# First pair reordered, third pair's words on ScalarE's queue, w_out's low bits through PSUM

## The chip, the cores and the metric

The kernel runs on one core of one Trainium2 chip. The metric is device time in microseconds of one execution; for the kernel before it is 912.71 us, the median of three runs (912.54 to 913.43). The engines are TensorE (PE, with its weight loads as PEld), VectorE (DVE), ScalarE (ACT), GpSimd (POOL) and SyncE (SP). SP and ACT also issue DMAs, each through a queue of its own.

## The reference, cut to what matters

Routed attention over 4 batches, 8 heads, 768 positions and 64 dimensions: each query and key is assigned to the nearest of 16 centroids of its head, and a query sees the keys of its own centroid only. Its output is the input of a two-layer block with a squared ReLU.

```python
q_assign = np.argmax(np.einsum('bhsd,hcd->bhsc', q_n, c_n), axis=-1)
k_assign = np.argmax(np.einsum('bhsd,hcd->bhsc', k_n, c_n), axis=-1)
mask = q_assign[:, :, :, None] == k_assign[:, :, None, :]
scores = np.where(mask, scale * np.matmul(q, k.transpose(0, 1, 3, 2)), -1e9)
x = attn @ v                       # bridge: (B,H,S,D) -> (3072, 512)
h = x @ w_in                       # 512 x 2048
out = np.square(np.maximum(h, 0)) @ w_out   # 2048 x 512
```

## The kernel before, in words

**Order.** Until the end of the first output tile the program is under a manual schedule: every engine works in the order in which the code is written, so the place of a call is its place in the engine's queue. A DMA issue stands in the queue of the engine that issues it, and waits there for what it needs.

**Attention.** Two heads make a pair, and 16 pairs (NG) are worked one after the other in the loop over `p`. For a pair, q and k are turned so that the head dimension lies on partitions (`qkT`), logits against the centroids give a number for each position, and these become rows (`ohT`) that a matmul turns into the mask. A pair has nine tiles: `mask` (L435) and `score` (L426) accumulate in one PSUM tile, `exponential` (L442) reads it on ScalarE, VectorE adds the tiles into `total` (L445), and `times_v` (L459) multiplies by v into the banks V and M (`av_a`, `av_b`). `add_up` (L478) sums `total` for the normalization. PSUM holds three `sc` tiles of two banks each, plus V and M.

How q and k are turned differs. Pairs 0 and 1 are turned on TensorE (L265 in `turn_first`, L282 in `turn`, with ScalarE and VectorE copying out of PSUM). From pair 2 on, `split_words` (L302) copies q and k on ScalarE into `flat`, a DMA (L303) writes them to DRAM as words, and a transposing DMA (L314, `turn_words`) brings them back. Pair 0 also has its one-hot rows turned on TensorE (L386 in `turn_onehot`), copied by ScalarE (L394) and VectorE (L396); later pairs send their numbers through DRAM (L370, L373) into `rows`, two buffers that are filled with zeros at the start (L218).

**Head.** Loads are issued first: pair 0's q on SP and its k on ACT behind the centroids, then pairs 1 and 2 and v on SP. GpSimd makes an identity, TensorE runs eight warm-up matmuls on it (L171), VectorE makes small constants and fills, `centroids_norm` (L226 to L245) prepares the centroids, pair 0 is turned, `centroids_turned` (L251, L254) turns the centroids, and the logits follow (L322).

**The two products.** The batches are worked in the order 1, 2, 3, 0. `up` multiplies by w_in: eight tiles of rows of the hidden layer, each with seven products (L742, four records each) by a Strassen-like scheme. `combine` runs them in the order 1, 6, 2, 7, 5, 4, 3, each into a PSUM bank: the first is copied out by ScalarE (L705), the others are added by VectorE (L699) or subtracted (L522). The sums of w_in that the scheme needs, `w_s`, are made by GpSimd (L542, L522) two tiles ahead. `down` multiplies by w_out in the same manner (L794), three tiles of columns per batch.

**Rounding.** Each weight block of 128 x 512 is loaded as 64-bit words and rounded in three steps. `round_1` on ScalarE makes the absolute value (L130) and the low bits (L131), which it writes over the low half of the loaded words. `round_2` on VectorE joins sign and low bits (L137), limits the value (L140) and shifts (L144). `round_3` on GpSimd adds both (L152). Blocks 0 to 14 (w_in) are done in the attention loop, block 15 and the 16 blocks of w_out inside the first `up`, three per tile: `Rounding.prepare` issues `round_1` for the next tile's blocks behind the copy of a tile's first product, and `Rounding.between` issues `round_2` and `round_3` behind the additions of products 6, 7 and 3. `up` and `down` share eight PSUM banks (`banks`).

Of the kernel before, what the change touches and what calls it, by code (L numbers as in the profile page):

```python
# [25 lines left out]
def kernel(  # L26
# [101 lines left out]
    def round_1(i):  # L128
        dst, lo, hi = of_block(i)
        nc.scalar.activation(out=dst.bitcast(F32), in_=hi.bitcast(F32), func=ACT.Abs)  # L130
        nc.scalar.activation(  # L131
            out=lo.bitcast(F32), in_=lo, func=ACT.Copy, bias=2.0, scale=2.0 ** -51
        )

    def round_2(i):
        dst, lo, hi = of_block(i)
        nc.vector.scalar_tensor_tensor(  # L137
            out=lo, in0=hi, scalar=0x80000000, in1=lo, op0=ALU.bitwise_and, op1=ALU.bitwise_or
        )
        nc.vector.tensor_scalar(  # L140
            out=hi.bitcast(F32), in0=dst.bitcast(F32), scalar1=2.0 ** -15, scalar2=HIGHEST,
            op0=ALU.max, op1=ALU.min,
        )
        nc.vector.tensor_scalar(  # L144
            out=dst, in0=hi, scalar1=3, scalar2=None, op0=ALU.logical_shift_left
        )
# [9 lines left out]
    load_qk(0, (nc.sync, nc.scalar))  # L156
    for pair in range(1, BY_PE + 1):
        load_qk(pair)
# [7 lines left out]

    ident = const.tile([P, P], F32, name="ident")
    make_identity(nc, ident)
    warm_up = ps_sc.tile([P, 2, 512], F32, name="sc")
    for _ in range(8):  # L170
        nc.tensor.matmul(warm_up[:, 0, 0:P], lhsT=ident, rhs=ident, start=True, stop=True)  # L171
# [45 lines left out]
    for t in rows_of:  # L217
        nc.vector.memset(t, 0.0)  # L218
# [31 lines left out]
    def centroids_turned():  # L250
        nc.tensor.transpose(  # L251
            out=M[:, 0:P], in_=cn.rearrange("p e d -> p (e d)"), identity=ident
        )
        nc.vector.tensor_copy(out=cnT, in_=M[:, 0:P])  # L254
# [4 lines left out]
    def turn_first(which):  # L259
        if which == 0:  # L260
            qkT[0] = qktp.tile([P, 2 * NCH, P], F32, name="qkT")
        pt = ps_sc.tile([P, 2, 512], F32, name="sc")
        for c in range(NCH):
            for e in range(2):
                nc.tensor.matmul(  # L265
                    pt[D * e : D * (e + 1), c // NB, (c % NB) * P : (c % NB + 1) * P],
                    lhsT=raw[0][which][:, e, c], rhs=ident, start=True, stop=True,
                )
        for i in range(2):
            copy = nc.vector.tensor_copy if which and i else nc.scalar.copy  # L270
            c = NCH * which + NB * i
            copy(out=qkT[0][:, c : c + NB].rearrange("p c n -> p (c n)"), in_=pt[:, i, 0:TB])
        if which == 1:
            raw.pop(0)
# [19 lines left out]
    def split_words(pair, which):  # L294
        if pair >= NG:
            return
        if which == 0:
            words[pair] = dram.tile([2 * NCH, P, 2, 2 * D], U16, name="words")
        flat = loads.tile([P, NCH, 2, 2 * D], U16, name="flat", tag="qk")
        src = raw[pair][which].bitcast(U16).rearrange("p h c (d two) -> p h c two d", two=2)  # L300
        for e in range(2):
            nc.scalar.copy(out=flat[:, :, :, D * e : D * (e + 1)], in_=src[:, e])  # L302
        nc.sync.dma_start(  # L303
            words[pair][NCH * which : NCH * (which + 1)].rearrange("c p two d -> p c two d"),
            flat,
        )
        if which == 1:
            raw.pop(pair)
# [69 lines left out]
    def turn_onehot():  # L378
# [4 lines left out]
        po = sc.pop("oh").rearrange("p a n -> p (a n)").bitcast(BF16)[:, 0 : NBL * P]  # L383
        po = po.rearrange("p (b g i) -> p b g i", b=NBL, g=4)
        for b in range(NBL):
            nc.tensor.transpose(  # L386
                out=po[:, b].rearrange("p g i -> p (g i)"),
                in_=oh[:, b].rearrange("p e c -> p (e c)"), identity=ident_b,
            )
        for which in range(2):  # L390
            dst = ohT[0][:, which].rearrange("p (g b i) -> p b g i", g=2, b=NBL)
            src = po[:, :, 2 * which : 2 * which + 2]
            if which == 0:
                nc.scalar.copy(out=dst, in_=src)  # L394
            else:
                nc.vector.tensor_scalar(  # L396
                    out=dst, in0=src, scalar1=BIG, scalar2=-BIG, op0=ALU.mult, op1=ALU.add
                )

# [164 lines left out]
    turn_first(0)  # L564
    turn_first(1)
    centroids_turned()
    logits(0, begin("ls"))
# [7 lines left out]
    for p in range(NG):  # L575
# [17 lines left out]
        if p == 0:  # L593
# [3 lines left out]
            split_words(2, 0)  # L597
            turn_onehot()
            turn(1, 2, V)
# [20 lines left out]
        if p == 0:  # L620
            split_words(2, 1)
            turn_words(2)
        split_words(p + 3, 0)
# [8 lines left out]
        if p:  # L632
            finish(p - 1)
            round_2(p - 1)
            round_3(p - 1)
        split_words(p + 3, 1)
# [30 lines left out]
    banks = fast.enter_context(tc.tile_pool(name="banks", bufs=8, space=PSUM, reuse_waits="tile"))  # L667
# [161 lines left out]
    class Rounding:  # L829
# [5 lines left out]
        def prepare(self, i):  # L835
            for n in self.of(i) + self.of(1) if i == 0 else self.of(i + 1):
                if n >= N_IN:
                    round_1(n)

        def between(self, i, j):  # L840
            n = dict(zip((6, 7, 3), self.of(i))).get(j)
            if n is not None:
                round_2(n)
                round_3(n)
                load_ahead(n + 1)
            elif (i, j) in SUMS:
# [221 lines left out]
```

## Time and profile before

| | |
|---|---|
| median of three runs | 912.71 us (912.54 to 913.43) |
| profiled execution: its own time, its span | 913.43 us, 911.6 us |
| PE busy | 899.4 us of the span |
| DVE, ACT, POOL busy | 581.7, 316.2, 150.1 us |
| logits of pair 0 (L322) | start at 10.09 us |
| first mask (L435) | starts at 17.49 us |
| first up (L742) | 321.44 to 398.83 us |
| a later up | 471.66 to 543.90 us |

Times of events count from the start of the span, which is that of one profiled execution; the span leaves out what lies around the first and the last instruction. A row of the timeline gives the start and the duration in us, the engine, the line, what is written from what, and in brackets how long the engine had been idle before and what ended it. Granted TensorE clock is 1.000 in the records of the whole span; the spacing of matmuls shows speed directly.

### The profile page before, as it was taken

The numbers are of one execution on the slowest core, as the hardware profiler recorded it, in microseconds if no ns is written. First come the engines' busy times: TensorE is split into PE (matmuls) and PEld (weight loads), VectorE is DVE, ScalarE is ACT, GpSimd is POOL, SyncE is SP. The second block draws the span as 40 slices with busy tenths as digits, with TensorE's granted clock in tenths as the row PEclk, the third lists the DMA queues.
The fourth block names the chain that finished last, engine by engine and source line by source line (L and its number), as shares of the span: only waits on it lengthen the run. The fifth ranks groups of instructions, "written<-read, shape, count | busy, mean of one in ns | idle before, by whom it ended". The sixth has DMA issues, their size and how long they took to land.

```text
span 911.6 us, 11728 instructions
## 1 busy us (share of the span) xinstructions
PE 899.4 (99%) x4543; PEld 578.8 (63%) x4543; DVE 581.7 (64%) x930; ACT 316.2 (35%) x457; POOL 150.1 (16%) x168
## 2 busy tenths in 40 slices
PE   8999999999999999899999999999999999999997
PEld 5444444444444455478875568886558887557886
DVE  5798888888888999994326565225655333656321
ACT  5876677776776567530001110001110000111000
POOL 0000100001000267710023310023220003240000
PEclk9999999999999999999999999999999999999999
DMA  7677778777673154110000000000000000000000
GB/s 261 154 191 220 218 214 208 179 210 213 172 177 86 61 184 139 41 70 24 24 24 0 1 0 19 18 19 16 1 1 0 24 24 24 0 1 0 24 24 27
DMA packets 98482, 75.03 MB, mean 82 GB/s; under 512 B 54666, under 2 KB 89074, under 8 KB 98162
## 3 DMA queue, kind: packets, MB, share of 16 engines
q1 hardware_dynamic: 91474, 64.33, 24.9%
q10 hardware_dynamic: 6944, 9.86, 3.4%
q8 instruction: 38, 0.62, 0.3%
q14 instruction: 26, 0.21, 0.1%
HBM read 43.83 MB, written 19.34 MB: 69 GB/s over the span
## 4 chain that ended last, share of the span: by engine, by line
PE 92%; DVE 5%; issue 1%; ACT 1%; POOL 0%; DVEq 0%; POOLq 0%
PE bank L794 32%; PE bank L742 28%; PE sc L426 12%; PE av_a L459 9%; PE av_b L459 4%; PE sc L435 3%; PE sc L322 1%; DVE w_raw L137 1%; PE sc L478 1%; DVE g L699 1%; DVE w_raw L140 1%; DVE total L445 1%; DVE xT L510 0%; PE sc L171 0%; PE sc L265 0%
## 5 line engine op out<-in xcount | busy, mean ns | idle before, releaser
L699 DVE TENSOR_TENSOR g<-bank,g 128x384 f32<-128x384 f32 x192 | 102.9, 553 | 90.8 <-PE bank L742 88.6
L442 ACT ACTIVATE ex<-sc 128x1024 f32<-128x1024 f32 x144 | 144.2, 1025 | 39.0 <-PE sc L426 34.1
L426 PE MATMUL sc<-qkT 64*128 64x512 f32 (+1 forms) x768 | 150.6, 484 | 0.0
L794 PE MATMUL bank<-w_out,g 128*128 128x256 f32 x576 | 127.2, 379 | 0.0
L794 PEld LDWEIGHTS bank<-w_out,g 128*128 128x128 f32 x576 | 109.4, 190 | 15.7
L699 DVE TENSOR_TENSOR osb<-bank,osb 128x256 f32<-128x256 f32 x72 | 29.3, 422 | 136.5 <-PE bank L794 125.9
L742 PE MATMUL bank<-x_t,w_s 128*128 128x384 f32 x256 | 93.3, 487 | 3.1 <-POOL w_s L522 3.1
L742 PE MATMUL bank<-xT,w_in 128*128 128x384 f32 x256 | 93.2, 487 | 0.0
L742 PE MATMUL bank<-xT,w_s 128*128 128x384 f32 x256 | 93.0, 486 | 0.0
L426 PEld LDWEIGHTS sc<-qkT 64*128 64x128 f32 x768 | 65.9, 188 | 41.9 <-issue 30.1
L794 PE MATMUL bank<-w_t,g_s 128*128 128x256 f32 x384 | 86.8, 379 | 0.0
L794 PE MATMUL bank<-w_t,g 128*128 128x256 f32 x384 | 86.8, 379 | 0.0
L459 PE MATMUL av_a<-ex,v_raw 128*64 128x512 f32 x384 | 85.9, 596 | 0.0
L542 POOL TENSOR_TENSOR w_s<-w_in 128x256 f32<-128x256 f32 x32 | 26.7, 835 | 351.3 <-PE bank L794 235.4
L445 DVE TENSOR_TENSOR total<-total,ex 128x1024 f32<-128x1024 f32 x64 | 78.7, 1229 | 6.5
L705 ACT COPY osb<-bank 128x256 f32<-128x256 f32 x12 | 4.5, 372 | 216.1 <-PE bank L794 216.1
L794 PEld LDWEIGHTS bank<-w_t,g_s 128*128 128x128 f32 x384 | 73.0, 190 | 9.9
L794 PEld LDWEIGHTS bank<-w_t,g 128*128 128x128 f32 x384 | 73.0, 190 | 9.9
L705 ACT COPY g<-bank 128x384 f32<-128x384 f32 x32 | 15.3, 477 | 173.9 <-PE bank L742 173.9
L742 PEld LDWEIGHTS bank<-x_t,w_s 128*128 128x128 f32 x256 | 48.4, 190 | 37.9 <-POOL w_s L522 4.8
L152 POOL TENSOR_TENSOR w_in<-w_in,w_raw 128x512 int32<-128x512 int32 x16 | 22.1, 1378 | 296.4 <-DVE w_in L144 296.4
L742 PEld LDWEIGHTS bank<-xT,w_s 128*128 128x128 f32 x256 | 48.6, 190 | 33.9
(128 smaller groups left out, 1021.5 us busy)
## 6 DMA issues: line engine op xcount, KB each, us to landing
words<-flat SPq DMA_DIRECT2D x28, 384.0 KB
w_raw<-in_moe_w_in_dram SPq DMA_DIRECT2D x16, 512.0 KB
w_raw<-in_moe_w_out_dram SPq DMA_DIRECT2D x16, 512.0 KB
v_raw<-in_v_dram SPq DMA_DIRECT2D x16, 384.0 KB
rb<-far_r SPq DMA_DIRECT2D x32, 192.0 KB
out_dram<-osb SPq DMA_DIRECT2D x23, 256.0 KB
k_raw<-in_k_dram ACTq DMA_DIRECT2D x13, 384.0 KB
q_raw<-in_q_dram ACTq DMA_DIRECT2D x12, 384.0 KB
```

Source lines behind the costliest of these rows:

```text
L137: nc.vector.scalar_tensor_tensor(out=lo, in0=hi, scalar=0x80000000, in1=lo, op0=ALU.bitwise_and, op1=ALU.bitwise_or)
L152: nc.gpsimd.tensor_tensor(out=dst, in0=dst, in1=lo, op=ALU.add)
L426: nc.tensor.matmul(sc[i][:, e, cols], lhsT=qkT[pair][rows, NCH + c], rhs=qkT[pair][rows, n.start // P : n.stop // P], start=first, stop=no ...
L435: nc.tensor.matmul(sc[i][:, e, cols], lhsT=ohT[pair][rows, 1, c * P : (c + 1) * P], rhs=ohT[pair][rows, 0, columns(i)], start=first, stop= ...
L442: nc.scalar.activation(out=ex[i], in_=sc.pop(i), func=ACT.Exp, scale=SCALE)
L445: eng.tensor_tensor(out=out, in0=a, in1=b, op=ALU.add)
L459: nc.tensor.matmul(bank[D * e : D * (e + 1), 0 : n.stop - n.start], lhsT=raw_v[pair][:, e, c], rhs=ex[i][:, e, cols], start=c == 0, stop=c ...
L542: nc.gpsimd.tensor_tensor(out=s1, in0=a[1][0], in1=a[1][1], op=ALU.add)
L699: nc.vector.tensor_tensor(out=out, in0=bank, in1=to, op=ALU.add)
L705: nc.scalar.copy(out=c11, in_=bank)
L742: nc.tensor.matmul(bank, lhsT=operands[j][0][:, kk], rhs=operands[j][1][:, kk], start=(kk == 0), stop=(kk == H2 - 1),)
L794: nc.tensor.matmul(bank, lhsT=left[:, f], rhs=right[:, f], start=(f == 0), stop=(f == F2 - 1))
```

## The change

- Loads: pair 0's k is issued on SP behind its q; ACT issues only the centroids there.
- Warm-up: six matmuls on a tile of zeros that VectorE fills, before the identity is made.
- Turning of pair 0: in four halves with a bank for each (V, M, and one of each of two `sc` tiles), the centroids' turning between the two halves of k.
- Fills of `rows`: moved behind `turn_onehot` on VectorE.
- One-hot rows: two halves in two banks, the first copied out by ScalarE for both q and k, the second by VectorE.
- Pair 2's words: both copies behind the first six exponentials, their DMAs issued by ACT; pair 3's first half moves behind the last three exponentials of pair 0.
- w_out's low bits: written by ScalarE into a tile of a pool of two PSUM banks (`lows`), read there by `round_2`; the bits of block n + 2 are issued behind `round_3` of block n. Six banks are left in `banks`.

```diff
--- before.py
+++ after.py
@@ -125,17 +125,26 @@
         dst = weights[i][0] if i < N_IN else w_out[:, i - N_IN]
         return dst.bitcast(U32), raw_w[i][:, :, 0], raw_w[i][:, :, 1]
 
-    def round_1(i):
+
+    low = {}
+
+    def round_1(i, bits=True):
         dst, lo, hi = of_block(i)
         nc.scalar.activation(out=dst.bitcast(F32), in_=hi.bitcast(F32), func=ACT.Abs)
+        if bits:
+            round_bits(i, lo.bitcast(F32))
+
+    def round_bits(i, out):
+        low[i] = out
         nc.scalar.activation(
-            out=lo.bitcast(F32), in_=lo, func=ACT.Copy, bias=2.0, scale=2.0 ** -51
+            out=out, in_=of_block(i)[1], func=ACT.Copy, bias=2.0, scale=2.0 ** -51
         )
 
     def round_2(i):
         dst, lo, hi = of_block(i)
         nc.vector.scalar_tensor_tensor(
-            out=lo, in0=hi, scalar=0x80000000, in1=lo, op0=ALU.bitwise_and, op1=ALU.bitwise_or
+            out=lo, in0=hi, scalar=0x80000000, in1=low.pop(i).bitcast(U32),
+            op0=ALU.bitwise_and, op1=ALU.bitwise_or,
         )
         nc.vector.tensor_scalar(
             out=hi.bitcast(F32), in0=dst.bitcast(F32), scalar1=2.0 ** -15, scalar2=HIGHEST,
@@ -153,8 +162,7 @@
 
     cen = once.tile([P, D], F32, name="cen")
     nc.scalar.dma_start(cen, centroids.rearrange("h c d -> (h c) d"))
-    load_qk(0, (nc.sync, nc.scalar))
-    for pair in range(1, BY_PE + 1):
+    for pair in range(BY_PE + 1):
         load_qk(pair)
     load_v(0)
 
@@ -164,11 +172,13 @@
         tc.manual_schedule(engines={E.PE, E.DVE, E.Activation, E.Pool, E.SP})
     )
 
+    zeros = once.tile([P, P], F32, name="zeros")
+    nc.vector.memset(zeros, 0.0)
+    warm_up = ps_sc.tile([P, 2, 512], F32, name="sc")
+    for _ in range(6):
+        nc.tensor.matmul(warm_up[:, 0, 0:P], lhsT=zeros, rhs=zeros, start=True, stop=True)
     ident = const.tile([P, P], F32, name="ident")
     make_identity(nc, ident)
-    warm_up = ps_sc.tile([P, 2, 512], F32, name="sc")
-    for _ in range(8):
-        nc.tensor.matmul(warm_up[:, 0, 0:P], lhsT=ident, rhs=ident, start=True, stop=True)
     ident_b = const.tile([P, P], BF16, name="ident_b")
     nc.vector.tensor_copy(out=ident_b, in_=ident)
     ups = const.tile([P, D], F32, name="ups")
@@ -214,8 +224,6 @@
     marks = once.tile([P, 3, 32], BF16, name="marks")
     nc.vector.memset(marks, 0.0)
     rows_of = [once.tile([P, 2, S], BF16, name=f"rows_{i}") for i in range(2)]
-    for t in rows_of:
-        nc.vector.memset(t, 0.0)
 
     cnT = const.tile([P, H * C], F32, name="cnT")
     cn = const.tile([P, 2, D], F32, name="cen_n")
@@ -248,29 +256,28 @@
             )
 
     def centroids_turned():
+        turned = warm_up[:, 1, 0:P]
         nc.tensor.transpose(
-            out=M[:, 0:P], in_=cn.rearrange("p e d -> p (e d)"), identity=ident
-        )
-        nc.vector.tensor_copy(out=cnT, in_=M[:, 0:P])
+            out=turned, in_=cn.rearrange("p e d -> p (e d)"), identity=ident
+        )
+        nc.vector.tensor_copy(out=cnT, in_=turned)
 
     qkT = {}
     ohT = {}
 
-    def turn_first(which):
-        if which == 0:
+
+    def turn_first(which, i, bank, copy):
+        if which == 0 and i == 0:
             qkT[0] = qktp.tile([P, 2 * NCH, P], F32, name="qkT")
-        pt = ps_sc.tile([P, 2, 512], F32, name="sc")
-        for c in range(NCH):
+        for c in range(NB):
             for e in range(2):
                 nc.tensor.matmul(
-                    pt[D * e : D * (e + 1), c // NB, (c % NB) * P : (c % NB + 1) * P],
-                    lhsT=raw[0][which][:, e, c], rhs=ident, start=True, stop=True,
+                    bank[D * e : D * (e + 1), c * P : (c + 1) * P],
+                    lhsT=raw[0][which][:, e, NB * i + c], rhs=ident, start=True, stop=True,
                 )
-        for i in range(2):
-            copy = nc.vector.tensor_copy if which and i else nc.scalar.copy
-            c = NCH * which + NB * i
-            copy(out=qkT[0][:, c : c + NB].rearrange("p c n -> p (c n)"), in_=pt[:, i, 0:TB])
-        if which == 1:
+        c = NCH * which + NB * i
+        copy(out=qkT[0][:, c : c + NB].rearrange("p c n -> p (c n)"), in_=bank[:, 0:TB])
+        if which == 1 and i == 1:
             raw.pop(0)
 
     def turn(pair, part, bank):
@@ -291,7 +298,7 @@
 
     words = {}
 
-    def split_words(pair, which):
+    def split_words(pair, which, queue=nc.sync):
         if pair >= NG:
             return
         if which == 0:
@@ -300,7 +307,7 @@
         src = raw[pair][which].bitcast(U16).rearrange("p h c (d two) -> p h c two d", two=2)
         for e in range(2):
             nc.scalar.copy(out=flat[:, :, :, D * e : D * (e + 1)], in_=src[:, e])
-        nc.sync.dma_start(
+        queue.dma_start(
             words[pair][NCH * which : NCH * (which + 1)].rearrange("c p two d -> p c two d"),
             flat,
         )
@@ -380,22 +387,30 @@
         ohT[0] = spare.rearrange("p a n -> p (a n)")[:, 0 : 2 * S].rearrange(
             "p (a n) -> p a n", a=2
         )
-        po = sc.pop("oh").rearrange("p a n -> p (a n)").bitcast(BF16)[:, 0 : NBL * P]
-        po = po.rearrange("p (b g i) -> p b g i", b=NBL, g=4)
-        for b in range(NBL):
-            nc.tensor.transpose(
-                out=po[:, b].rearrange("p g i -> p (g i)"),
-                in_=oh[:, b].rearrange("p e c -> p (e c)"), identity=ident_b,
-            )
-        for which in range(2):
-            dst = ohT[0][:, which].rearrange("p (g b i) -> p b g i", g=2, b=NBL)
-            src = po[:, :, 2 * which : 2 * which + 2]
-            if which == 0:
-                nc.scalar.copy(out=dst, in_=src)
-            else:
-                nc.vector.tensor_scalar(
-                    out=dst, in0=src, scalar1=BIG, scalar2=-BIG, op0=ALU.mult, op1=ALU.add
+
+        for half, bank in enumerate((sc.pop("oh")[:, 0], M)):
+            n = NBL // 2
+            blocks = slice(n * half, n * (half + 1))
+            po = bank.bitcast(BF16)[:, 0 : n * P].rearrange("p (b g i) -> p b g i", b=n, g=4)
+            for b in range(n):
+                nc.tensor.transpose(
+                    out=po[:, b].rearrange("p g i -> p (g i)"),
+                    in_=oh[:, n * half + b].rearrange("p e c -> p (e c)"), identity=ident_b,
                 )
+            for which in range(2):
+                dst = ohT[0][:, which].rearrange("p (g b i) -> p b g i", g=2, b=NBL)[:, blocks]
+                src = po[:, :, 2 * which : 2 * which + 2]
+                if half == 0:
+                    nc.scalar.activation(
+                        out=dst, in_=src, func=ACT.Copy,
+                        **({"scale": BIG, "bias": -BIG} if which else {}),
+                    )
+                elif which:
+                    nc.vector.tensor_scalar(
+                        out=dst, in0=src, scalar1=BIG, scalar2=-BIG, op0=ALU.mult, op1=ALU.add
+                    )
+                else:
+                    nc.vector.tensor_copy(out=dst, in_=src)
 
 
 
@@ -561,9 +576,12 @@
             loaded += 1
 
     centroids_norm()
-    turn_first(0)
-    turn_first(1)
+    turn_first(0, 0, V, nc.scalar.copy)
+    turn_first(0, 1, M, nc.scalar.copy)
+    halves = [ps_sc.tile([P, 2, 512], F32, name="sc")[:, 0] for _ in range(2)]
+    turn_first(1, 0, halves[0], nc.scalar.copy)
     centroids_turned()
+    turn_first(1, 1, halves[1], nc.vector.tensor_copy)
     logits(0, begin("ls"))
     for i in ("oh", 0, 1):
         begin(i)
@@ -594,8 +612,9 @@
             for i in range(2):
                 turn(1, i, (V, M)[i])
                 score(p, i, 0, True)
-            split_words(2, 0)
             turn_onehot()
+            for t in rows_of:
+                nc.vector.memset(t, 0.0)
             turn(1, 2, V)
             for i in range(NB):
                 if i == 2:
@@ -618,9 +637,11 @@
             tile_of(p, i)
             add(nc.vector, first, first, ex[i])
         if p == 0:
-            split_words(2, 1)
+            for i in range(2):
+                split_words(2, i, nc.scalar)
             turn_words(2)
-        split_words(p + 3, 0)
+        else:
+            split_words(p + 3, 0)
 
 
         for i in range(NCH, NCH + NB):
@@ -633,6 +654,8 @@
             finish(p - 1)
             round_2(p - 1)
             round_3(p - 1)
+        if p == 0:
+            split_words(3, 0)
         split_words(p + 3, 1)
         load_qk(p + 4, (nc.scalar, nc.scalar))
         round_1(p)
@@ -664,7 +687,8 @@
 
     w_out = w_out_pool.tile([P, FT, DM], F32, name="w_out")
     fast = ExitStack()
-    banks = fast.enter_context(tc.tile_pool(name="banks", bufs=8, space=PSUM, reuse_waits="tile"))
+    banks = fast.enter_context(tc.tile_pool(name="banks", bufs=6, space=PSUM, reuse_waits="tile"))
+    lows = fast.enter_context(tc.tile_pool(name="lows", bufs=2, space=PSUM, reuse_waits="tile"))
     outp = fast.enter_context(tc.tile_pool(name="outp", bufs=2, reuse_waits="tile"))
     gp = fast.enter_context(tc.tile_pool(name="gp", bufs=1, reuse_waits="tile"))
 
@@ -835,7 +859,13 @@
         def prepare(self, i):
             for n in self.of(i) + self.of(1) if i == 0 else self.of(i + 1):
                 if n >= N_IN:
-                    round_1(n)
+                    round_1(n, False)
+                    if n < N_IN + 2:
+                        self.bits(n)
+
+        def bits(self, n):
+            if n < N_IN + FT:
+                round_bits(n, lows.tile([P, NW], F32, name="low"))
 
         def between(self, i, j):
             n = dict(zip((6, 7, 3), self.of(i))).get(j)
@@ -843,6 +873,8 @@
                 round_2(n)
                 round_3(n)
                 load_ahead(n + 1)
+                if n >= N_IN:
+                    self.bits(n + 2)
             elif (i, j) in SUMS:
                 w_out_sum(SUMS[i, j])
 
```

## The prediction

> **What bounds the kernel now.** I read the page first, then the chain of waits, then the timeline of the two stretches that the diff touches.
>
> ```profile
> PE 899.4 (99%) x4543; PEld 578.8 (63%) x4543; DVE 581.7 (64%) x930; ACT 316.2 (35%) x457; POOL 150.1 (16%) x168
> ...
> PE 92%; DVE 5%; issue 1%; ACT 1%; POOL 0%; DVEq 0%; POOLq 0%
> ```
>
> TensorE is busy for 899.4 of 911.6 us, so an edit elsewhere pays only where TensorE stands still, or runs slowly. The chain of waits shows the first such stretch, the head:
>
> ```profile
> 1.36 3.78 PE sc L171 x16
> 5.14 3.51 PE sc L265 x48
> 8.68 0.49 ACT qkT L272
> 9.19 0.56 DVE qkT L272
> 9.74 0.21 DVE cnT L254
> ...
> 10.09 0.85 PE sc L322 x8
> ...
> 14.58 1.57 ACT flat L302 x2
> 16.14 0.71 ACT ex L394
> 16.88 0.57 DVE ex L396
> 17.49 0.61 PE sc L435 x4
> ```
>
> Warm-up, turning of the first pair, copies and logits (L322) follow one another; then ScalarE's two copies of L302 stand ahead of the one-hot copy that the first mask (L435) waits for. From 17.49 on, the chain stays on TensorE with only short issue gaps.
>
> The second stretch is the first w_in product (up), from 321.44 to 398.83 us. The chain gives a later one as its measure:
>
> ```profile
> 471.66 72.24 PE bank L742 x224
> ```
>
> The first takes 398.83 - 321.44 = 77.39 us, 0.78 of it L478, so it loses 77.39 - 0.78 - 72.24 = 4.4 us. The timeline shows how:
>
> ```profile
> 378.46 1.28 POOL L152 TENSOR_TENSOR w_out<-w_out,w_raw 128x512 int32<-128x512 int32 x1 [2.09 <-DVE w_out L144]
> 378.76 1.53 DVE L137 SCALAR_TENSOR_TENSOR w_raw<-w_raw 128x512 uint32<-128x512 uint32 x1
> 378.89 1.45 PE L742 MATMUL bank<-xT,w_in 128*128 128x384 f32 x4
> 379.70 1.17 POOL L542 TENSOR_TENSOR w_s<-w_in 128x256 f32<-128x256 f32 x1
> 380.33 0.83 DVE L140 TENSOR_SCALAR w_raw<-w_out 128x512 f32<-128x512 f32 x1
> ...
> 381.79 1.56 PE L742 MATMUL bank<-x_t,w_s 128*128 128x384 f32 x4 [1.45 <-POOL w_s L522]
> ```
>
> L137 takes 0.68 us where GpSimd is idle, and 1.53 here beside L152; L140 takes 0.43 alone and 0.83 here. VectorE and GpSimd hold each other up, w_s comes late, and TensorE waits (two waits, 3.1 us in all).
>
> **The change, part by part: warm-up and first turning.** TensorE now multiplies zeros that VectorE fills, not the identity that GpSimd makes (wait until 1.36). The other engines' first work begins at 0.74; a fill like L175 takes 0.11 us, so TensorE can start near 0.95. The 16 passes of L171 took 3.78 us, 0.236 each; six matmuls are 12 passes, 2.83 us, and end at 3.8. By slices of 0.1 us, the queue of the first q load carries its last packet between 3.7 and 3.8. So the old warm-up kept TensorE away from data that was there for 1.3 us, and the new one ends as it arrives. I let the turning start at 3.9.
>
> Clock: L265's passes come 0.105 us apart until about 6.3 (five us after TensorE began) and the 24 of k 0.062 apart. With the switch left at 6.3, q's 24 passes end at 6.4. The k half is 12 x 0.062 = 0.74, to 7.14; the centroids' transpose to about 7.4; the other half to 8.14. **A rule speaks against this:** the Trainium skill (TensorE: Matmul & The Clock Gate, Part 1) says that full clock needs about 3.4 us of sustained work seen through a free-running window, however many matmuls that is. By it the switch may come anywhere from 3.4 to 6.8 us after the start at 0.95, that is 4.4 to 7.8. By the row I keep 6.3; the late end costs (7.8 - 6.3)/2 = 0.75 us, the early end gains up to about 0.8. No run here shows the window itself.
>
> The k load moves from ScalarE's queue to second place on SP's. All loads together ran at about 390 GB/s, so one of 384 KB takes 1.0 us: k is there by about 4.9, needed at 6.4; pair one's q by 5.9, k 6.9, pair two's 7.9 and 8.9, v 9.9, needed at 24. All are hidden, a late k having 1.5 us of room.
>
> The two fills of L218 (1.50 us, before 4.87) leave VectorE's head, so the centroids' chain (4.79 to 7.87) starts near 3.4 and ends near 6.5, wanted at 7.14. The fills now follow the one-hot copies, where VectorE sat idle for 2.46 us; without that cover they would cost 1.5. The last k copy on VectorE is 0.56: 8.2 to 8.76. Logits of the first three groups run meanwhile, the last ends at 9.0; before it ended at 10.94. Gain so far 1.94.
>
> **One-hot rows.** After the logits TensorE has 4.1 us of turning and scores (10.94 to 15.04), now 9.0 to 13.1. VectorE's row numbers, ready at 14.53 before, are ready near 12.6, so TensorE does not wait. The 12 transposes take 0.84 us, to 13.95, the last turning 1.09, to 15.1. ScalarE no longer has L302 in front: its two half copies, about 0.45 each by half of L394's 0.80, run 13.6 to 14.5 and VectorE's two 14.0 to 14.8; the new wait of the second half is on bank M's copy, done near 12.8. The mask starts at 15.1, not 17.49: **2.4 us**.
>
> **Third pair's words.** Both L302 pairs (1.57 us each) now follow the first six exponentials, near 22, each with an issue of about 0.4 us in ScalarE's own queue, where that issue waits for its copy and holds the later copies and exponentials: last exponential at about 29.0. The second v product reads it after 31, and the sums of VectorE (L445, 1.2 each) fit ahead of L478 at 32.0. The fourth pair's copies come behind, then two weight roundings and the evictions; the next pair's first exponential then starts near 34.35 for a tile ready at 34.0, and a third PSUM buffer gives 0.85 us of room before TensorE would stop. Without that room it costs 0.4. The transpose L314 was issued at 33.17 and its reader L322 came at 38.57; now words end near 29 and the reader comes at 36.2. On SP the far and rows transfers lose the words issue ahead of them. Cost zero, bound 0 to 0.8.
>
> **w_out's low bits.** ScalarE writes them to PSUM, so L137 reads one operand from PSUM. No row shows this operation. The nearest is L699, also PSUM with SBUF: 0.55 us at 367.53, beside L152 from 367.69 to 368.99, so undisturbed. The skill (SBUF — State Buffer, Who interferes with whom) has the same line: two SBUF inputs contend with GpSimd, one does not; but a copy or tensor_scalar in a two-port mode still does, and the loser blocks fully. By the rule's first half alone, L137's excess over 0.68, summed over blocks 16 to 31, is 6.1 us of VectorE time. By the rows, L140 inherits much: at 378.76 L137 would end at 379.44, and L140 would then wait for L152. Bounds for L137: 0.68 to 1.55; I take 0.68, by L699.
>
> Against it stand two new waits. Two banks go to the bits, so TensorE may run six products ahead, not eight; already with eight it once waited 0.6 us for VectorE. And ScalarE's copy of a tile's first product is queued behind the bits of two blocks on, which wait for L137 of the tile's last block; the tile's first addition on VectorE waits for both: about 0.4 us per tile. I walked tiles 1 to 5 with L137 at 0.68, L140 and L144 at 0.43 plus their waits, L152 at 1.29 and L542/L522 at 0.73, taking turns. VectorE reaches the first addition of tile 3 at 357.1 (before 357.94), of tile 4 at 366.5 (367.53), of tile 5 at 376.85 (378.29). With six banks TensorE then stops for about 0.9, 0.4, 1.25 and 1.25 us and starts tile 7 at 389.6; it started at 389.63. So gain and loss meet: **zero**. If VectorE were no faster, the same walk puts tile 7 about 2.3 us later; if the banks never ran out, 2.5 earlier. In later products VectorE trails by one product or two and six banks are enough.
>
> **Sum:** -2.4 in the head, 0 in the rest. Against the profiled execution (span 911.6, its time 913.43, 0.72 over the median): span 909.2, time 911.0; median 912.71 - 2.4 = 910.3.
>
> **The rivals.**
> 1. *VectorE's relief shows, banks suffice* (chance 0.2): L140 waits less than walked, L742 loses 1 to 2.5 us less. For: six collisions of 0.85 us. Against: L140's own waits. Time near 908.5.
> 2. *Head gain only in part, or eaten by first up* (0.3): late clock (+0.75), a stop in pair one (+0.4), banks (+0.5 to 1.5). Time near 911.8, within 0.2% (1.8 us, about what a measurement of this kernel can tell from no change).
> 3. *Six banks make the first up slower* (0.1): L137 collides as before, and the wait on the bits delays VectorE by 0.4 in each of five tiles. Place: tiles 3 to 6; price 2.3 + 2.0 = 4.3, less 2.4: +1.9, 914.6. It decides once VectorE trails by over five products (5 x 1.29 = 6.45 us); before, it trailed by 6.3 at tile 4. Against: the L699 row.
> 4. *The low bits do nothing*: covered by the forecast, whose term is zero.
>
> **How the numbers follow.** Forecast (0.4): 910.3, its own range 909.5 to 911.3. Rival 1 ends faster, the forecast faster in about 0.36 of its 0.4, rival 2 in 0.05 of its 0.3. So faster by over 0.2% 0.61; slower 0.09, most of rival 3; same 0.30. Range from rival 1's best part to a little over no change: 907.8 to 913.0.
>
> **What would show it.** First mask near 15.1 us, and no gap on TensorE before it over 0.2; warm-up from 0.95; the first up still near 77 us, with TensorE waiting for VectorE's additions in place of w_s; L137 at 0.68 throughout. Wrong: a first up under 75 or over 79, L137 still at 1.5, or passes of 0.105 us in k's turning.

## The result, and the profile after

The median after is 910.16 us (908.56 to 912.03 in eight runs), against 912.70 for the kernel before (912.28 to 914.03): ratio 0.9971, interval 0.9959 to 0.9982. The forecast was 910.3. The total agrees; what it is made of does not, as the traces and the runs show.

The profiled execution of after is the fastest of its eight: 908.56 us, span 906.8. The experiments below add a second profile, of an execution of 913.27 us. Both are needed. The page of the first one, 908.56 us, engines and then the chain's shares:

```profile
PE 898.5 (99%) x4539; PEld 577.6 (64%) x4539; DVE 576.4 (64%) x932; ACT 315.7 (35%) x458; POOL 146.8 (16%) x168
...
PE 94%; DVE 4%; issue 1%; DMA 0%; ACT 0%; DVEq 0%
```

TensorE still bounds the kernel, its busy time is 0.9 us less, and VectorE has lost 5.3 us of work. POOL has left the chain. The head, in the chain of waits of the same execution (start, duration, what):

```profile
0.74 3.59 DMA q_raw<-in_q_dram
4.33 0.14 issue
4.47 0.98 PE av_a L274 x12
5.45 0.66 PE av_b L274 x12
6.10 0.66 PE sc L274 x12
6.76 0.26 PE sc L260
7.02 0.81 PE sc L274 x12
7.82 1.49 PE sc L329 x8
```

The warm-up is gone from the chain; in its place stands the load of q, which TensorE waits for until 4.47. The first 12 passes of the turning take 0.98, the next 0.66: TensorE has sped up within the first. The first mask (L450) starts at 15.21; it was 17.49.

In the first up, VectorE's groups of w_out blocks between 325 and 385 us (count | busy us, mean ns | idle before):

```profile
L149 DVE TENSOR_SCALAR w_raw<-w_out 128x512 f32<-128x512 f32 x16 | 11.5, 716 | 0.5
L145 DVE SCALAR_TENSOR_TENSOR w_raw<-w_raw,low 128x512 uint32<-128x512 uint32 x16 | 10.8, 677 | 0.0
```

and all stops of TensorE from 318 to 400 us, in its timeline:

```profile
369.83 1.53 PE L766 MATMUL bank<-xT,w_s 128*128 128x384 f32 x4 [0.24 <-DVE g L723]
379.73 1.53 PE L766 MATMUL bank<-xT,w_s 128*128 128x384 f32 x4 [0.63 <-DVE g L723]
```

L145 (L137 before) now takes 0.677 us in every block. TensorE no longer waits for w_s; two short waits for VectorE's additions are left, 0.87 us where the two waits for w_s were 3.15. The first up runs from 319.39 to 394.16, 74.77 us; it was 77.39.

So this execution is 4.8 us of span better: 2.05 at the start of the first up, 2.62 in it, 0.1 behind. The median says 2.5. The question is where the rest of the head's gain goes in the other executions.

### The profile page after: what moved, and what is told of

The parts are those of the page before. It is cut to its first block, busy times and chain, and to the rows that moved or that the text cites. A ratio compares the mean times of both kernels' runs of the same rounds, so it can differ in the third digit from the quotient of the medians.

```text
span 906.8 us, 11735 instructions
## 1 busy us (share of the span) xinstructions
PE 898.5 (99%) x4539; PEld 577.6 (64%) x4539; DVE 576.4 (64%) x932; ACT 315.7 (35%) x458; POOL 146.8 (16%) x168
## 4 chain that ended last, share of the span: by engine, by line
PE 94%; DVE 4%; issue 1%; DMA 0%; ACT 0%; DVEq 0%
PE bank L818 32%; PE bank L766 29%; PE sc L441 13%; PE av_a L474 9%; PE av_b L474 4%; PE sc L450 3%; PE sc L329 1%; PE sc L493 1%; DVE g L723 1%; DVE total L460 1%; DVE w_raw L149 1%; DVE w_raw L145 1%; DVE xT L525 0%; DMA q_raw<-in_q_dram 0%; DVE x_t L537 0%
## 5 line engine op out<-in xcount | busy, mean ns | idle before, releaser
L766 PEld LDWEIGHTS bank<-xT,w_in 128*128 128x128 f32 x256 | 48.5, 190 | 33.8 <-DVE g L537 0.6
```

The costliest lines, as they stand in the source:

```text
L766: nc.tensor.matmul(bank, lhsT=operands[j][0][:, kk], rhs=operands[j][1][:, kk], start=(kk == 0), stop=(kk == H2 - 1),)
```

## The experiments

Ratios are to the kernel before on the same chip; a few slow runs move them more than they move the medians. The median of before was 912.8 in the first group, 913.2 in the second and 913.3 in the third.

| kernel | median us | ratio, interval | first mask | logits of pair 2 | first up: start, length |
|---|---|---|---|---|---|
| before (profile shown) | 912.70 | | 17.49 | 38.57 | 321.44, 77.39 |
| after (first profile) | 910.16 | 0.9971 (0.9959-0.9982) | 15.21 | 36.47 | 319.39, 74.77 |
| head_only | 912.66 | 1.0011 (0.9997-1.0024) | 16.27 | 37.78 | 320.72, 77.41 |
| bits_only | 910.01 | 0.9969 (0.9958-0.9981) | 17.39 | 38.71 | 321.65, 74.79 |
| head_six_banks | 915.36 | 1.0035 (1.0023-1.0047) | 15.69 | 37.88 | 320.82, 79.79 |
| bits_in_sbuf | 914.99 | 1.0028 (1.0017-1.0040) | 15.09 | 37.67 | 320.62, 79.81 |
| late_loads | 908.57 | 0.9950 (0.9937-0.9963) | 15.20 | 36.45 | 319.33, 74.76 |
| seven_banks | 912.08 | 0.9996 (0.9980-1.0012) | 15.54 | 37.31 | 320.26, 77.08 |
| late7_both | 911.55 | 0.9978 (0.9968-0.9987) | 14.96 | 36.21 | 319.08, 77.01 |
| words_before | 909.16 | 0.9955 (0.9942-0.9967) | 15.56 | 36.76 | 319.71, 74.78 |
| late_head | 911.43 | 0.9980 (0.9971-0.9989) | 14.97 | 36.23 | 319.11, 77.34 |
| after_again (one run) | 913.27 | | 15.55 | 39.25 | 323.83, 74.78 |
| before_again (one run) | 913.07 | | 17.42 | 38.50 | 321.38, 77.41 |
| bits_again (one run) | 910.93 | | 17.75 | 38.83 | 321.72, 74.79 |

### Each half alone

**head_only**: loads, warm-up, turning, fills, one-hot rows and words as after; low bits and eight banks as before.

```diff
-        out=lo, in0=hi, scalar=0x80000000, in1=low.pop(i).bitcast(U32), ...
+        out=lo, in0=hi, scalar=0x80000000, in1=lo, ...
-    banks = ... bufs=6 ...
-    lows = ... bufs=2 ...
+    banks = ... bufs=8 ...
```

> All edits of the attention head (loads, warm-up, turning, fills, one-hot halves, third pair's words), w_out's low bits as before, eight banks. Theory 1 (the head alone makes the change, low bits sum to about zero): 2.1 us under the kernel before, first mask at 15.2 us, first up 76 to 77 us long. Theory 2 (part of the head's gain is lost again later, the low bits make the rest): under 1 us, with a first up longer than 77.

**bits_only**: the head as before; low bits in PSUM and six banks as after.

```diff
-    for pair in range(BY_PE + 1):
+    load_qk(0, (nc.sync, nc.scalar))
+    for pair in range(1, BY_PE + 1):
         load_qk(pair)
...
-    for _ in range(6):
-        nc.tensor.matmul(warm_up[:, 0, 0:P], lhsT=zeros, rhs=zeros, ...)
+    for _ in range(8):
+        nc.tensor.matmul(warm_up[:, 0, 0:P], lhsT=ident, rhs=ident, ...)
...
-            for i in range(2):
-                split_words(2, i, nc.scalar)
+            split_words(2, 1)
             turn_words(2)
```

> Head as before; low bits in two PSUM banks, six banks for the products. Theory 1: within 1 us of the kernel before; first up 76 to 77.5 us. Theory 2 (the profile after shows a first up that is 2.6 us shorter, and that is the rule): 1.5 to 2.6 us faster, first up near 75 with TensorE stopped only by two or three late additions.

The low bits alone bring all that the whole change brings (0.9969 and 0.9971), the head alone nothing that this many runs can tell from no change (1.0011). That is the reverse of the forecast's sum. Yet head_only's mask starts 1.22 us earlier than before's, and part of that is gone later. Its chain of waits has a place where it can go:

```profile
29.73 7.91 DMA qkT<-words
37.64 0.14 issue
37.78 0.85 PE sc L320 x8
```

The transposing DMA of pair 2's words starts at 29.73, 3.4 us earlier than before (33.17), but takes 7.9 us to land, and TensorE waits for it before the logits of pair 2:

```profile
37.78 0.85 PE L320 MATMUL sc<-qkT,cnT 128*32 128x384 f32 x8 [0.26 <-DMA qkT<-words]
```

In this execution the wait is short, 0.26 us. Of the 1.22 us at the mask 0.79 are left at the logits of pair 2 and 0.72 at the first up, and the mask itself comes 1.06 later than in the profile of after, since TensorE sped up later in the head (below). So this profile names a suspect; what it costs, the next runs must show.

### What the low bits are made of

**head_six_banks**: head_only with six banks and no PSUM tile for the bits.

```diff
-    banks = ... bufs=8 ...
+    banks = ... bufs=6 ...
```

> As head_only, with six banks instead of eight and the low bits still over the loaded words in SBUF; two banks lie idle. The walk of the prediction says that VectorE's old timing and six banks end the first up 2.3 us later: so about 2.3 us slower than head_only, near the kernel before. The other theory (TensorE waits for w_s anyhow, and banks take that wait over): within 0.5 us of head_only.

**bits_in_sbuf**: after, but the bits go over the loaded words in SBUF; order and six banks stay.

```diff
-                round_bits(n, lows.tile([P, NW], F32, name="low"))
+                round_bits(n, of_block(n)[1].bitcast(F32))
```

> As the changed kernel in every order and with six banks, but the low bits are written over the loaded words in SBUF, so L137's form (two operands in SBUF) returns. If it is the PSUM operand that pays: collisions of L137 with GpSimd return (up to 1.55 us each), first up 2 to 4.3 us longer than the changed kernel's, about 1 to 2 us slower than the kernel before. If the later issue of the bits pays and not the place: as the changed kernel within 1 us.

The three steps of the edit separate in the length of the first up, which hardly varies between executions (74.76 to 74.79 in six profiles with two PSUM banks for the bits, 77.34 to 77.41 in four with the bits in SBUF and eight banks). Six banks cost 79.79 - 77.41 = **+2.38**. The later order of the bits costs 79.81 - 79.79 = **0.02**. The PSUM operand brings 74.77 - 79.81 = **-5.04**. In whole times the last is 0.9971 against 1.0028, 0.6% or 5.2 us. (A tile of its own for the bits in SBUF was not tried.) The stops of TensorE with six banks and no relief, head_six_banks, timeline:

```profile
360.88 1.53 PE L756 MATMUL bank<-x_t,w_s 128*128 128x384 f32 x4 [1.42 <-POOL w_s L528]
364.66 1.53 PE L756 MATMUL bank<-xT,w_s 128*128 128x384 f32 x4 [0.96 <-DVE g L713]
375.44 1.53 PE L756 MATMUL bank<-xT,w_s 128*128 128x384 f32 x4 [1.36 <-DVE g L713]
386.19 1.53 PE L756 MATMUL bank<-xT,w_s 128*128 128x384 f32 x4 [1.36 <-DVE g L713]
```

and VectorE's groups in bits_in_sbuf, same view and window as for after above:

```profile
L145 DVE SCALAR_TENSOR_TENSOR w_raw<-w_raw 128x512 uint32<-128x512 uint32 x16 | 17.0, 1065 | 0.0
L149 DVE TENSOR_SCALAR w_raw<-w_out 128x512 f32<-128x512 f32 x16 | 11.8, 740 | 0.5
```

With one operand in PSUM, L145 falls from 17.0 to 10.8 us over 16 blocks, and L149, which the prediction let inherit the wait for GpSimd, does not rise: 11.8 and 11.5. VectorE keeps the whole 6.2 us.

### Where the head's gain goes

**late_loads**: after, with one line changed. In pair 0 the loads of pair 4's q and k, which ACT issued at 27.44 and 28.88 in after, are issued by SP behind pair 2's transpose and pair 3's words.

```diff
-        load_qk(p + 4, (nc.scalar, nc.scalar))
+        load_qk(p + 4, (nc.scalar, nc.scalar) if p else (nc.sync, nc.sync))
```

> The kernel after the change, but in pair 0 the loads of pair 4's q and k are issued by SP behind the transposing DMA of pair 2's words and the words of pair 3, not by ACT. Theory (the head's gain is lost since these loads share the DMA engines with the transposing DMA): the transposing DMA takes about 5 us from its start instead of 8 to 9, ends near 34, the logits of pair 2 wait for nothing, and the second pair's sum with v starts near 43.9 in every run: 908.0 to 908.8, 1.5 to 2 us below the kernel after (910.2), with a small spread. Rival (the transposing DMA is slow by itself when it is issued that early, or the words come too late): it still takes 8 us, and the time is that of the kernel after, 910. A third way: the loads come too late for pair 4's words, and a later pair stops: over 910.5.

It is as the theory said: 908.57, all five runs within 0.8 us, the logits of pair 2 at 36.45 without a wait. SP's timeline shows the transposing DMA's issue, 3.09 us long:

```profile
28.67 3.09 SPq L321 DMA_TRANSPOSE qkT<-words  x1
31.87 1.18 SPq L310 DMA_DIRECT2D words<-flat  x2
33.10 1.66 SPq L89 DMA_DIRECT2D q_raw<-in_q_dram  x1
```

**words_before**: after, with the order of pair 2's words as before.

```diff
             for i in range(2):
                 turn(1, i, (V, M)[i])
                 score(p, i, 0, True)
+            split_words(2, 0)
             turn_onehot()
...
         if p == 0:
-            for i in range(2):
-                split_words(2, i, nc.scalar)
+            split_words(2, 1)
             turn_words(2)
-        else:
-            split_words(p + 3, 0)
+        split_words(p + 3, 0)
...
-        if p == 0:
-            split_words(3, 0)
         split_words(p + 3, 1)
```

> The kernel after the change, but pair 2's words as in the kernel before: the first half's copies and issue ahead of the one-hot rows, the second half issued by SP, pair 3's first half right behind. Theory: ScalarE's two copies (1.57 us) again hold up the one-hot copy and the first mask starts 0.8 to 1.6 us later, near 16.5; the transposing DMA starts later and runs after pair 4's loads, in about 3 to 5 us, and the logits of pair 2 come without a wait: what the move of the words gained at the mask, it lost at the transposing DMA, so the time is that of the kernel after within 0.5, about 910. Rival (the words' move is all of the head's gain): the time is 911 or more. Rival (the words' move is the loss): under 909.3.

The outcome is the second rival's: the move of the words is the loss, 909.16. Its interval and that of after overlap, so the times alone do not settle it; the trace shows both sides of the move. In the chain, ScalarE's copies of L309 stand again ahead of the one-hot copy:

```profile
12.71 0.46 issue
13.16 1.57 ACT flat L309 x2
14.73 0.78 ACT ex L404 x2
15.56 0.61 PE sc L450 x4
```

and hardly matter: from the first logits to the mask it is 15.56 - 8.04 = 7.52 us here and 15.21 - 7.82 = 7.39 in after. The move was worth 0.13 us at the mask. The loads of pair 4 are issued at 24.95 and 26.52 here, since the first copies free ScalarE's queue earlier, and the transposing DMA at 31.62 finds no packets of ACT's queue beside it: its issue takes 2.83. The loads stay on ACT's queue in this run, which speaks for the overlap, and not the queue, as what costs.

**late_head**: head_only with the one line of late_loads.

> The head's edits alone (the low bits as in the kernel before, eight banks), with pair 4's first loads issued late by SP. Theory (the head's edits are worth what the mask gained, once the collision of the loads with the transposing DMA is gone): the logits of pair 2 wait for nothing and the time falls from 912.7 (head alone) to 910.5 to 911.2. Rival (the later loads gained elsewhere in the kernel with both edits): it stays near 912.7.

0.9980 against head_only's 1.0011, intervals apart: one line is worth 1.7 us by the medians (1.84 under before against 0.15), and 0.3% or 2.8 us by the ratios, on which head_only's slowest runs weigh. The two profiles alone would not show it: of the 1.55 us between their logits of pair 2 (37.78 and 36.23) 1.30 are there at the mask, before the line that differs has an effect, and only 0.25 are the wait.

What the other executions pay shows in the spread. Of the 36 runs of head_only, head_six_banks, bits_in_sbuf and seven_banks, whose loads of pair 4 all overlap with the transposing DMA, eight lie more than 2 us above the median of their kernel, head_only's up to 918.51. Of the 36 runs of bits_only, words_before, late_loads, late7_both and late_head, where those loads come before it or queue behind it, none does. (None of after's eight runs does either; its second profile, below, is 2.5 us above where its median would lie in that group.) None of the eight was profiled, so what they pay is not split into stop and clock.

The median of 911.43 lies 0.2 above the expected range on a chip where before was 913.3 and not 912.8; as a ratio it is 1.84 us under before, and the starts of the first up (319.11 against 321.38 in before_again) differ by 2.27. So the head's edits are worth about 2 us once the collision is gone, a little less than the 2.4 forecast. With bits_only the sum is 0.31 + 0.20 = 0.51%, and late_loads, which has both, measures 0.50%.

**after_again, before_again, bits_again**: the kernels unchanged, for a second profile each.

> The kernel after, for a second profile: the one that was read is the fastest of its eight runs. Theory: an execution near 910.2 has the mask again near 15.3, and TensorE waits 0.2 to 1.3 us for the transposing DMA before the logits of pair 2, which start 37.4 or later and not 36.47. Rival: no wait there, and the 1.6 us lie in the first up.

> The kernel before, for a second profile. The prediction set its head against an execution that lay 0.72 above the median. Theory (the excess lies in the head, where the warm-up or TensorE's clock came late): with a time near 912.7 the first mask starts near 16.8 and not 17.49, and the first up near 320.8 and not 321.44. Rival (the excess lies elsewhere): the mask again at 17.5.

> The low bits alone, for a second profile: the first was 0.9 above the median of its runs. Theory: an execution near 910.0 has its first up at about 74.8 us as before, and starts it 0.9 earlier, near 320.7; the 0.9 lie in pair 1, where the transposing DMA was waited for. Rival: they lie in the first up.

The second execution of after took 913.27 us, and shows the highest price of all profiles. Its chain:

```profile
26.18 2.83 DMA words<-flat
29.06 10.05 DMA qkT<-words
39.11 0.14 issue
39.25 1.13 PE sc L329 x8
40.37 0.54 PE sc L450 x2
40.92 1.71 PE sc L441 x4
```

The transposing DMA lands ten us after its start, TensorE stands for 2.44 us, and then runs slowly: a score of four matmuls takes 1.71 us, where the same at 44.21 takes 0.86. The stretches of the same execution give the reason (stretch and length in us; busy time of PE, PEld, DVE, ACT and POOL; granted clock; share and GB/s of the DMA engines). The granted clock falls to 0.50:

```profile
39.00:40.00 1.00, 0.75 (x8) 0.19 (x8) 0.00 (x0) 0.00 (x0) 0.00 (x0) 0.85 1.05 318
40.00:41.00 1.00, 1.00 (x8) 0.61 (x6) 0.58 (x1) 0.00 (x0) 0.00 (x0) 0.50 0.91 288
41.00:42.00 1.00, 1.00 (x4) 0.20 (x4) 0.93 (x2) 0.00 (x0) 0.00 (x0) 0.50 0.13 18
42.00:43.00 1.00, 1.00 (x6) 0.50 (x4) 0.93 (x3) 0.33 (x1) 0.00 (x0) 0.50 0.11 26
43.00:44.00 1.00, 1.00 (x8) 0.43 (x6) 0.93 (x5) 0.69 (x1) 0.00 (x0) 0.94 1.01 99
```

From the logits to the product with v it is 48.33 - 39.25 = 9.08 us, against 43.89 - 36.47 = 7.42 in the first profile of after. So 4.44 us of later first up are 0.34 in the mask, 2.44 of stop and 1.66 of clock. One kernel, two executions, and all but 0.34 us of the difference lies in pair 1.

What the queues did at the same moment: DMA packets from 32 to 34 us in after_again (queue: packets, MB, share of the engines' time; q10 is ACT's queue with the loads, q1 is SP's with the transposing DMA):

```profile
q10 hardware_dynamic: 114, 0.18, 77.7%
q1 hardware_dynamic: 126, 0.03, 17.7%
```

and in late_loads, in the same two microseconds:

```profile
q1 hardware_dynamic: 1227, 0.31, 123.2%
```

In these two microseconds the two queues get about equal numbers of packets, but those of the loads carry 1.6 KB each and those of the transposing DMA 256 B, so the latter moves 0.03 MB where it moves 0.31 alone. The Trainium skill (DMA: Bandwidth & Descriptors, Queues, rings and completion order) has each DMA engine take turns between the rows that have work, a packet at a time. The counts 126 and 114 would fit, but in the two microseconds before they are 329 and 148, and in the first profile of after, from 30 to 32 us, 372 and 139; equal turns are not shown here. They would not be all, either: together they moved 0.21 MB, less than either alone, and the transposing DMA stays slow when the loads are over: from 36 to 37 us ACT's queue has 8 packets left, and SP's moves 247; in the next microsecond it moves 1134. Why is not shown.

The other two missed what was expected of them. The second execution of before (913.07) has its mask at 17.42 and its first up 0.06 us from the first profile's start, so that the 0.72 us by which the first profile lay above its median cannot be placed in the head. That of bits_only came out at 910.93 like the one before it, with no wait for the transposing DMA and the mask 0.36 later (17.75 against 17.39), and settles nothing about its runs at 910.0.

### Can TensorE's last two waits go?

**seven_banks**: after, with one PSUM bank for the bits and seven for the products, and the bits issued one block ahead.

```diff
-    banks = ... bufs=6 ...
-    lows = ... bufs=2 ...
+    banks = ... bufs=7 ...
+    lows = ... bufs=1 ...
...
-                    if n < N_IN + 2:
+                    if n < N_IN + 1:
                         self.bits(n)
...
-                    self.bits(n + 2)
+                    self.bits(n + 1)
```

> The kernel after the change, but the low bits have one PSUM bank and the products seven; the bits of block n + 1 are issued behind round_3 of block n. Theory (six banks cost 2.4 us in the first up when VectorE is slow, 0.9 now that it is faster): the two stops of 0.24 and 0.63 us go, the first up lasts 73.9 us and not 74.8: about 0.9 faster than the kernel after, near 909.3. Rival (with one bank the bits wait for the block before, and VectorE waits for the bits): L145 waits for ScalarE up to 1 us per block, the first up stays at 75 or more: 910 to 912.

**late7_both**: this and the line of late_loads.

> Both edits, the later loads of pair 4 and seven banks: if both theories hold the two gains add, since they lie in different stages: 907.2 to 908.2, about 5 us below the kernel before. If only one holds, its gain alone: 908.5 or 909.3.

The first up gets longer, 77.08 and 77.01 us; the rival is right. ScalarE's and VectorE's timeline in seven_banks:

```profile
347.38 1.78 ACT L133 ACTIVATE w_out<-w_raw 128x512 f32<-128x512 f32 x3
...
349.06 0.61 ACT L139 ACTIVATE low<-w_raw 128x512 f32<-128x512 uint32 x1
...
349.76 0.69 DVE L145 SCALAR_TENSOR_TENSOR w_raw<-w_raw,low 128x512 uint32<-128x512 uint32 x1 [2.20 <-POOL w_out L161]
```

Issued one block ahead, the bits stand in ScalarE's queue behind the squares of a whole tile and three absolute values (L133); they end at 349.67, and VectorE has waited 2.20 us. The row names POOL, but POOL's sum had ended at 349.16; what came last is ScalarE. Two banks are not spare room: they let the bits stand ahead of that batch. late7_both keeps the early logits of late_loads (36.21) and loses 2.25 us in the first up. So late_loads, with 908.57, is the best version of this study: 4.6 us under the kernel before.

## Why the prediction was right in its total and wrong in its parts

**Warm-up and data.** The warm-up starts at 1.06, not 0.95. I let the turning start at 3.9, since q's last packet comes by 3.8. TensorE waited to between 4.29 and 4.47, for 0.30 to 0.48 us, a gap that the prediction had ruled out. So some 0.5 us or more pass between the last packet and the release (an estimate: that last packet was read in the kernel before, the release in those after). Nor was q always there so early under the old order: in bits_only its load lands at 5.26. Missed by 0.5.

**Clock.** I kept the switch at 6.3 and priced an earlier or later one at 0.8 and 0.75. In the profile of after it comes near 4.8 (an estimate: its first 12 passes take 0.80 us from start to start, the next 12 0.65), 1.5 earlier, which made good the late data. It moves from run to run, as q's two halves show, first in head_only, then in late_head:

```profile
4.41 1.55 PE L265 MATMUL av_a<-ident,q_raw 128*64 128x128 f32 x12 [0.43 <-DMA q_raw<-in_q_dram]
5.72 1.44 PE L265 MATMUL av_b<-ident,q_raw 128*64 128x128 f32 x12
...
4.33 0.88 PE L265 MATMUL av_a<-ident,q_raw 128*64 128x128 f32 x12 [0.34 <-DMA q_raw<-in_q_dram]
5.00 0.85 PE L265 MATMUL av_b<-ident,q_raw 128*64 128x128 f32 x12
```

The first 12 passes take 1.31 us from start to start in head_only, 0.109 each, and k follows at 6.97, so nearly all of q is slow; in late_head they take 0.67, 0.056 each, fast from the first. That puts the switch anywhere from 4.3 or before to about 6.9; the prediction had named 4.4 to 7.8 as possible and kept 6.3. In the ten profiles with the new head the first logits start at 7.56 (late7_both) to 8.88 (head_only), and the mask at 14.96 to 16.27. That the mask came at 15.21 with a forecast of 15.1 is luck: late data and an early switch cancel.

**One-hot rows.** The two copies of L302 in front of the one-hot copy were read off the chain as what held the mask. words_before puts them back and loses 0.13. They were the last link of the chain, but with the one-hot copy in halves they nearly fit before it.

**Third pair's words: the step that failed.** "Cost zero, bound 0 to 0.8." The words land near 29 as I said. I then took the transposing DMA's time from the execution before, where it ran from 33.17 and its reader at 38.57 did not wait, and named no queue that it was moved past. It was moved by 4.5 us into the loads of pair 4, which ACT's queue carries from 27.5 to 34 in the first profile of after and to 36 in after_again. Its issue on SP, in before, after and after_again:

```profile
33.17 2.82 SPq L314 DMA_TRANSPOSE qkT<-words  x1
...
28.70 5.52 SPq L321 DMA_TRANSPOSE qkT<-words  x1
...
29.06 8.01 SPq L321 DMA_TRANSPOSE qkT<-words  x1
```

In place of 2.8 us it needs 5.5 to 8.0, and its landing can set the logits of pair 2. Cost: nothing in the first profile of after; waits of 0.26 us in head_only, 0.52 in seven_banks, 0.93 in head_six_banks and 1.32 in bits_in_sbuf; 4.1 us in after_again. The bound was too small by a factor of five, and the half clock behind a stop was not in it at all.

**Low bits: a term mis-sized.** L145 at 0.68 by the row of L699: it is 0.677. Six banks +2.3 by the walk's worst case: 2.38. ScalarE's coupling 0.4 per tile: three waits of 0.20. The relief was put at about 2.3, and is 5.04. The failed step is "L140 would then wait for L152": the walk handed most of the 6.1 us on to L140, whose total did not rise (11.8 us before, 11.5 after). The rule of the Trainium skill taken alone (SBUF — State Buffer, Who interferes with whom: two inputs in SBUF contend with GpSimd, one does not), which the working named and set aside as 6.1 us, had it right: 6.2 were measured. The walk had VectorE at tile 5's first addition 1.44 us earlier than before; counted from the start of the first up, it came 3.9 earlier (52.95 against 56.85).

**The sum.** -2.4 and 0 were forecast; the runs show -1.2 to -2.5 at the mask and -2.6 in the first up, and 0 to +4.1 in pair 1, by the execution. Both of the first two rivals came true, one for each half, and they offset each other: that 910.16 lies so near 910.3 is luck. Of the signs that were named as proof of an error, "a first up under 75" appeared, at 74.77. Without the second profile the total would have passed for a proof of the steps.

## What to carry to other kernels

When a DMA is moved earlier, look at what the other queues carry at its new time, not only at whether its data are ready: a transfer of small packets beside one of large packets took two to three times as long to issue here (5.5 and 8.0 us against 2.8), and one line that lets the large one wait gave back 1.6 us by the medians. Try PSUM for one operand of a VectorE instruction that runs beside GpSimd, and do not hand its gain on to the next instruction without a measurement: here the whole excess, 6.2 us, was gained. A total that agrees proves no part of the sum; undo each half, and profile a second execution when the first is the fastest of its runs.

## What was not expected of the hardware

- A stop of 2.44 us was enough for TensorE to fall to half its clock, 0.4 us after it had begun to work again, for 3.4 us (granted clock 0.50 from 39.7 to 43.1): 1.66 us on top of the stop. The Trainium skill (TensorE: Matmul & The Clock Gate, Why this matters for your kernels) warns of idle gaps over about 3 us; here a shorter one did it, while the stops of 0.26 to 1.32 us at the same place in four other kernels, and of 1.70 us in the first up of before, did not.
- In the head the passes are slow or fast by a factor of two (0.109 and 0.056 us each, head_only and late_head), while the records give the granted clock as 1.00 there. The spacing of the passes shows the switch, the column does not.
- The transposing DMA's slowness outlasts the loads that it collided with: in after_again it moved 247 packets from 36 to 37 us, with 8 of the loads' left, and 1134 in the next.
